# Attention and a maxout layer on one core: the first batch's queries in two parts, any free bank pair for any job, and a new order for every engine

## The chip, the cores and the metric

One NeuronCore of a Trainium2 chip. The five engines run their own instruction streams and wait for each other by semaphores: TensorE (PE) multiplies, ScalarE (ACT) takes exponentials, VectorE (DVE) moves, scales and transposes, GpSimd (POOL) casts, SyncE (SP) issues DMAs. The metric is device microseconds of one execution, lower is better.

## What is computed

Eight batches of eight heads, 1152 positions, head size 64. Queries are averaged in pairs, so 576 queries attend to 1152 keys. The result, 4608 tokens of 512 features, goes through a layer that takes the larger of two projections and projects back.

```python
q_pool = q.reshape(B, H, S // 2, 2, D).mean(axis=3)
scores = scale * np.matmul(q_pool, k.transpose(0, 1, 3, 2))
attn = softmax(scores)
attn_out = np.matmul(attn, v)
x = attn_out.transpose(0, 2, 1, 3).reshape(B * (S // 2), H * D)
g = np.maximum(x @ w1, x @ w2)
out = g @ w_out
```

Inputs and the output are float32; the kernel multiplies in bfloat16.

## The kernel before

**Attention.** A unit of work is a pair of heads: 8 batches x 4 = 32 head pairs, numbered 0 to 31. For each, queries are summed in pairs (`cast_q`, POOL), keys and values cast (`cast_k`, `cast_v`, POOL), and queries and keys transposed so that the head dimension lies on partitions. Keys of the first five pairs and queries of the first five are transposed by PE (`ktrans_pe`, `qtrans`, `qtrans0`) and copied out by VectorE; later keys by a DMA (`ktrans`), later queries by eight VectorE transposes (`qtrans_dve`). Scores are laid out as one long row of columns, pair after pair, key tile after key tile (9 tiles of 128 keys x 576 queries = 5184 columns, `PW`), and cut into groups of 512 columns: 324 groups, 10.125 a pair. `scores(g)` computes one group for both heads as row-tiled matmuls of 64 rows, which run side by side, into two PSUM banks, and ACT takes the exponential of both into `et` (line 591). When all groups of a pair are there, `av_jobs` multiplies them with the values: per head four chunks of 128 queries, nine matmuls each (line 495), and one remainder of 64 queries for both heads (line 507). A column of ones in the values gives the sum, VectorE divides (lines 517 to 525) into `xnat`, and `xtrans` (DMA) or `xtrans_pe` (PE, the first four pairs, the last of each batch in some stretches, and the last pair) transposes the result into `xT`.

**The layer.** max(a, b) = max(a - b, 0) + b, so the kernel forms `wd` = w1 - w2 (POOL), computes relu(x wd) (the h blocks, line 798 row-tiled in pairs of banks, line 771 singly at the end) and adds x (w2 w_out): `w21` = w2 w_out is made once on the chip (line 716) from w2 transposed by PE (line 687). The p blocks (lines 831 and 864) sum relu(x wd) w_out and x w21 for 128 or 256 tokens. An h block may begin only when all four head pairs of its tokens are in `xT`.

**Order.** A greedy planner (`choose`, `steady`, `refill` and a `table` of settings by time) makes the list of operations, with estimated costs. Then four strings written out by hand or by search (`pe_order` and so on, line 1413) give the order in which PE, VectorE, POOL and SP go through their lanes; `Plan.solve` places the semaphore waits. In `pe_order`, S is the next score group, a digit the next unit of the job in that PSUM bank, and y, z, Y, Z a fill: four dummy matmuls of 128 columns (line 319) that compute nothing that is used. There are 23 such letters, 7 of them at the start.

**PSUM.** Eight banks in four pairs. Scores use the three `sps` pairs in turn (`ring`) until the layer begins, then two of them; `fb` and the third `sps` pair hold the other jobs.

**First batch.** Pairs 0 to 3 are taken whole, one after the other. Only pair 0's queries are loaded and transposed in two parts, of 256 and 320 (`QA` = 256, `runs`):

```python
def runs(i):
    return ((0, QA), (QA, SQ)) if i == 0 else ((0, SQ),)
```

Of the kernel before, what the change touches and what calls it, by code (L numbers as in the profile page):

```python
# [7 lines left out]
P = 128  # L8
# [7 lines left out]

class Plan:

    INORDER = ("PE", "ACT", "DVE", "POOL")
    LAT = {"PE": 0.182, "ACT": 0.181, "DVE": 0.010, "POOL": 0.010}  # L20
    HEAR = {"PE": 0.046, "ACT": 0.024, "DVE": 0.024, "POOL": 0.075, "SP": 0.05}

    def __init__(self):
        self.ops = []
        self.writer = {}
        self.readers = {}
        self.free = {}
        self.dma_free = 0.0
        self.mode = None
        self.act_end = 0.0  # L30
        self.last = {}

    def deps(self, r, w, after=()):
        raw = {self.writer[k] for k in r if k in self.writer}
# [5 lines left out]
        return deps, raw  # L40

    def when(self, eng, r=(), w=(), after=(), fence=False):

        if any(k not in self.writer for k in r):
            return 1e9
        t = self.free.get(eng, 0.0)
        for d in self.deps(r, w, after)[0]:
            p = self.ops[d]
            if p["eng"] != eng or p["dma"] is not None or fence:
                t = max(t, p["seen"] + self.HEAR[eng])  # L50
        return t

    def op(self, eng, fn, r=(), w=(), dma=None, cost=0.1, mode="f", after=(), solo=False,
           fence=False):
        n = len(self.ops)
        assert all(k in self.writer for k in r), r
        deps, raw = self.deps(r, w, after)
        prev = self.last.get(eng)
        if prev is not None and (solo or self.ops[prev]["solo"]):
            deps.add(prev)  # L60
            raw.add(prev)
        self.last[eng] = n
        t = self.when(eng, r, w, after, fence)
        if dma is not None:
            if not self.dma_free:
                t = 0.78
            self.free[eng] = t + (1.3 if mode == "t" else 0.5)
            a = max(self.free[eng] + 1.2, self.dma_free)
            self.dma_free = a + cost + (0.9 if a < 5.0 <= a + cost else 0.0)
            seen = self.dma_free + 0.5  # L70
        else:
            if eng == "PE" and mode != self.mode:
                t = max(t, self.free.get("PE", 0.0) + 0.098)
                self.mode = mode
            busy = cost
            seen = t + cost + self.LAT[eng]
            if eng == "ACT":
                busy = cost + 0.051
                seen = max(seen, self.act_end + cost + 0.0735)
                self.act_end = seen  # L80
            elif eng == "DVE":
                busy = cost + 0.012
            self.free[eng] = t + busy
        self.ops.append(dict(eng=eng, fn=fn, deps=deps, raw=raw, dma=dma, w=tuple(w),
                             seen=seen, end=self.free[eng], solo=solo, fence=fence, r=tuple(r), at=n))
# [7 lines left out]
    def lane(self, o):  # L93
        key = (o["w"] or ("o",))[0]
        if o["eng"] == "PE":
            return "S" if key[0] == "s" else key[1:]
        if o["eng"] == "SP":
            return {"kT": "t"}.get(key[:2], key[0])
        if o["eng"] == "POOL":
            return {"kb": "k", "wd": "d"}.get(key[:2], key[0])  # L100
        for k in o["r"] + o["w"]:
            if k[0] == "f" and k[1:].isdigit():
                return k[1:]
        return {"qt": "T", "w2": "W", "wo": "W"}.get(key[:2], "Q")

    def reorder(self, want):

        ops = self.ops
        line = {}
        for n, o in enumerate(ops):  # L110
            line.setdefault(o["eng"], []).append(n)
        for eng, text in want.items():
            lanes = {}
            for n in line[eng]:
                lanes.setdefault(self.lane(ops[n]), []).append(n)
            assert sorted(c for c in text if c not in self.fill) == sorted(
                c for c, v in lanes.items() for _ in v)
            line[eng] = []
            for c in text:
                if c in self.fill:  # L120
                    m, mode, fn = self.fill[c]
                    key = f"f{m}"
                    nxt = ops[lanes[str(m)][0]]
                    n = len(ops)
                    ops.append(dict(
                        nxt, fn=fn, w=(key,), r=(), raw={self.writer["warm"]}, fence=False, at=n, inc=False, mode=mode, cost=0.0,
                        deps={d for d in nxt["deps"] if key in ops[d]["w"] and ops[d]["eng"] != eng}
                        | {self.writer["warm"]}))
                    nxt["deps"].add(n)
                    line[eng].append(n)  # L130
                else:
                    line[eng].append(lanes[c].pop(0))
        place = {}
        while len(place) < len(ops):
            before = len(place)
            for eng in line:
                while line[eng] and all(d in place for d in ops[line[eng][0]]["deps"]):
                    place[line[eng].pop(0)] = len(place)
            assert len(place) > before
# [5 lines left out]
    def solve(self):  # L145
# [3 lines left out]
        for n, o in enumerate(ops):  # L149
# [3 lines left out]
            for d in sorted(o["deps"], reverse=True):  # L153
                p = ops[d]
                if p["dma"] is None:
                    if p["eng"] == eng and not o["fence"] and (eng == "PE" or eng != "DVE" and d not in o["raw"]):
                        continue
# [29 lines left out]
    def emit(self, eng, h, sem, last_waits=()):  # L187
        for o in self.ops:
# [9 lines left out]
            inst = o["fn"](h)  # L198
# [8 lines left out]
class Job:  # L207


    def __init__(self, kind, units, evac, done=None, nb=None, single=None):  # L210
        self.kind, self.units, self.evac, self.done = kind, units, evac, done
        self.nb = nb
        self.single = single


def bass_funnel_attn__then__act_maxout2_kernel(
# [25 lines left out]
    assert NB == HP and NTOK % 512 == 0 and NT == 9 and B % 2 == 0  # L242
# [3 lines left out]
    NGR = NPAIR * PW // W  # L246

    ctx = ExitStack()
    with ctx:
# [6 lines left out]
        ident = sbuf([P, P], BF16, "ident")  # L256
        qraw = [sbuf([P, QU, 2, D], FP32, f"qraw{s}") for s in range(3)]
        kraw = [sbuf([P, 2, NT, D], FP32, f"kraw{s}") for s in range(3)]
        vraw = [sbuf([P, 2, NT, D], FP32, f"vraw{s}") for s in range(3)]
        qpw = [sbuf([P, QU, 2, D], BF16, f"qp{s}") for s in range(2)]  # L260
        qp = [t[0:HP, :, :, :] for t in qpw]
# [181 lines left out]
        def qtrans_dve(i, n):  # L443
# [9 lines left out]
            if n == 7:  # L453
                q_done.add(i)
# [1043 lines left out]
```

## Time and profile before

| what | value |
|---|---|
| median of three executions | 367.1 us (365.78, 367.1, 369.88) |
| profiled execution, span from first to last instruction | 368.9 us |
| exponentials, ACT | 307.6 us in 336 instructions |
| scores, PE | 121.5 us in 1162 matmuls |
| query transposes, VectorE | 101.3 us in 216 instructions |
| read from HBM, written | 62.91 MB, 9.44 MB |

The profile is of one execution on the chip. Busy times are unions of instructions on an engine; matmuls are pipelined and their ends are modelled, so a busy PE can still be one that loses time between matmuls. Views used below: the page's busy shares; windows, which give each engine's busy time within a stretch of the span; the timeline, in which neighbouring instructions of one kind are merged (start, length, engine, line, output and inputs, count); the waits; and the chain that ended last. The fill matmuls appear at line 319 and count as busy.

### The profile page before, as it was taken

What the parts mean: (1) busy time and instruction counts of PE and PEld (TensorE: products, weight loads), DVE (VectorE), ACT (ScalarE), POOL (GpSimd) and SP (SyncE); (2) the same over time, 40 slices, a digit from 0 to 9 for tenths busy, and PEclk for the clock granted to TensorE, in tenths of its full rate; (3) what the DMA queues carried; (4) which work ended last, traced back from release to release, by engine and by line L of the source; (5) the groups of instructions that cost most, each with busy time, mean ns of one, the idle gap of its engine ahead of it and who ended that gap; (6) DMA issues with size and microseconds to landing.
All of it is one profiled execution on the core that took longest, in us unless ns stands there. A gap on an engine that the chain in (4) does not pass through costs nothing.

```text
span 368.9 us, 13316 instructions
## 1 busy us (share of the span) xinstructions
PE 359.1 (97%) x5941; PEld 225.9 (61%) x5945; DVE 240.9 (65%) x521; ACT 315.6 (86%) x355; POOL 124.7 (34%) x111
## 2 busy tenths in 40 slices
PE   6999999999999999999999999999999999999996
PEld 5766564665556665657565665665666666556853
DVE  1478378867778867848885776577877766714411
ACT  4699989999999998999998999999999989895221
POOL 1256675533134333372242602525224440010000
PEclk9599999999999999999999999999999999999999
DMA  7999959999939998898999999998999680913206
GB/s 265 406 396 397 402 108 328 307 312 164 330 102 234 291 271 253 211 297 178 251 349 185 252 245 236 283 304 181 277 253 197 191 201 6 181 43 72 54 0 171
DMA packets 77640, 84.71 MB, mean 230 GB/s; under 512 B 49936, under 2 KB 50704, under 8 KB 77584
## 3 DMA queue, kind: packets, MB, share of 16 engines
q1 hardware_dynamic: 77024, 83.09, 84.8%
q8 instruction: 46, 0.75, 0.9%
q10 hardware_dynamic: 560, 0.79, 0.6%
q14 instruction: 10, 0.08, 0.1%
HBM read 62.91 MB, written 9.44 MB: 196 GB/s over the span
## 4 chain that ended last, share of the span: by engine, by line
PE 95%; DMA 2%; ACT 2%; issue 1%; SPq 0%; POOL 0%; DVE 0%; DVEq 0%
PE sps L584 22%; PE sps L495 12%; PE sps L831 11%; PE fb L831 10%; PE fb L495 9%; PE sps L798 8%; PE fb L798 7%; PE sps L864 3%; PE sps L507 2%; PE fb L716 2%; DMA kraw<-in_k_dram 2%; ACT et L591 2%; PE fb L507 1%; PE fb L864 1%; PE sps L771 1%; PE fb L319 1%
## 5 line engine op out<-in xcount | busy, mean ns | idle before, releaser
L591 ACT ACTIVATE et<-sps 128x1024 bf16<-128x1024 f32 (+1 forms) x336 | 307.6, 1002 | 25.1 <-PE sps L584 23.0
L584 PE MATMUL sps<-qpT,kT 64*128 64x256 bf16 (+7 forms) x1162 | 121.5, 287 | 1.0 <-issue 0.5
L449 DVE STREAM_TRANSPOSE qpT<-qp 32x288 bf16<-32x288 bf16 x216 | 101.3, 469 | 5.6 <-PE sps L584 1.5
L584 PEld LDWEIGHTS sps<-qpT,kT 64*128 64x128 bf16 x1162 | 49.6, 95 | 48.1 <-ACT et L591 15.8
L389 POOL TENSOR_TENSOR qp<-qraw 128x576 bf16<-128x576 f32 x30 | 42.1, 1406 | 98.2 <-DVE qpT L449 76.2
L395 POOL TENSOR_SCALAR vE<-vraw 128x1152 bf16<-128x1152 f32 x32 | 36.9, 1154 | 60.7 <-DMA vraw<-in_v_dram 60.7
L495 PE MATMUL sps<-vE,et 128*128 128x65 bf16 x1368 | 48.4, 193 | 0.0
L495 PEld LDWEIGHTS sps<-vE,et 128*128 128x128 bf16 x1368 | 43.6, 97 | 6.0 <-issue 5.3
L356 POOL TENSOR_SCALAR kbf<-kraw 128x1152 bf16<-128x1152 f32 x31 | 35.7, 1153 | 33.5 <-DMA kT<-kbf 16.5
L798 PE MATMUL sps<-xT,wd 64*128 64x512 bf16 (+3 forms) x368 | 43.7, 326 | 0.0
L831 PE MATMUL sps<-wo,stage 64*128 64x512 bf16 x256 | 36.8, 376 | 0.0
L495 PE MATMUL fb<-vE,et 128*128 128x65 bf16 x936 | 33.5, 193 | 0.5 <-issue 0.5
L798 PE MATMUL fb<-xT,wd 64*128 64x512 bf16 (+3 forms) x272 | 33.6, 333 | 0.1
L495 PEld LDWEIGHTS fb<-vE,et 128*128 128x128 bf16 x936 | 29.9, 97 | 5.5 <-issue 4.8
L831 PE MATMUL fb<-wo,stage 64*128 64x512 bf16 x224 | 33.0, 376 | 0.0
L807 DVE TENSOR_SCALAR stage<-sps 128x1024 bf16<-128x1024 f32 (+3 forms) x23 | 22.3, 969 | 15.7 <-PE sps L798 15.6
L798 PEld LDWEIGHTS sps<-xT,wd 64*128 64x128 bf16 x368 | 15.6, 94 | 13.7 <-PE sps L798 1.4
L807 DVE TENSOR_SCALAR stage<-fb 128x1024 bf16<-128x1024 f32 (+3 forms) x17 | 17.0, 999 | 10.7 <-PE fb L798 10.4
L517 DVE RECIPROCAL rc<-sps 128x5 f32<-128x5 f32 (+1 forms) x38 | 7.1, 186 | 19.7 <-PE sps L495 19.2
L831 PE MATMUL sps<-w,xT 64*128 64x512 bf16 x128 | 18.7, 377 | 0.0
L842 DVE COPY stage<-sps 128x1024 f32<-128x1024 f32 x8 | 9.8, 1225 | 12.8 <-PE sps L831 12.7
L831 PEld LDWEIGHTS sps<-wo,stage 64*128 64x128 bf16 x256 | 12.1, 94 | 9.5
(81 smaller groups left out, 296.6 us busy)
## 6 DMA issues: line engine op xcount, KB each, us to landing
vraw<-in_v_dram SPq DMA_DIRECT2D x32, 576.0 KB, 6.6
kraw<-in_k_dram SPq DMA_DIRECT2D x31, 576.0 KB, 6.6
qraw<-in_q_dram SPq DMA_DIRECT2D x31, 576.0 KB, 6.7
out_dram<-stage SPq DMA_DIRECT2D x21, 256.0 KB, 5.5
out_dram<-stage SPq DMA_DIRECT2D x23, 128.0 KB, 3.2
xT<-in_moe_w_dram SPq DMA_DIRECT2D x4, 512.0 KB, 10.7
stage<-in_moe_w_out_dram SPq DMA_DIRECT2D x4, 512.0 KB, 13.5
stage<-in_moe_w_dram SPq DMA_DIRECT2D x4, 512.0 KB, 13.1
```

Source lines behind the costliest of these rows:

```text
L356: op("POOL", lambda g: g.tensor_scalar(kbf[s][:, :, :, :].rearrange("p t h d -> p h t d"), kraw[r][:, :, :, :], 1.0, 1.0, ALU.mult, ALU.mu ...
L389: op("POOL", lambda g: g.tensor_tensor(qpf[s][:, :, :], qraw[r][:, :, 0, :], qraw[r][:, :, 1, :], ALU.add), r=[f"qraw{r}"], w=[f"qp{s}.0", ...
L395: op("POOL", lambda g: g.tensor_scalar(vE[r][:, :, :, 0:D].rearrange("p t h d -> p h t d"), vraw[r][:, :, :, :], 1.0, 1.0, ALU.mult, ALU.m ...
L449: op("DVE", lambda e: e.transpose(view[dst:dst + 32, :, 32 * pb:32 * pb + 32], qpf[s][src:src + 32, :, 32 * db:32 * db + 32]), r=[f"qp{s}. ...
L495: last = e.matmul(fb[m][:, sb * 66:sb * 66 + 65], et[:, a:a + P], vE[vs][:, t, half, 0:65], start=(t == 0), stop=(t == NT - 1))
L507: last = e.matmul(fb[m][rows(half), NCH * 66:NCH * 66 + 65], et[:, a:a + NB], vE[vs][:, t, half, 0:65], start=(t == 0), stop=(t == NT - 1))
L584: last = e.matmul(sps[r][:, h, col:col + hi - lo], kT[i % 3][rows(h), t, :], qpT[i % 3][rows(h), lo:hi], start=True, stop=True)
L591: op("ACT", lambda e: e.activation(et2[:, :, c:c + z - a], sps[r][:, :, a - g * W:z - g * W], EXP, scale=scale), r=[f"s{r}"], w=keys + ([f ...
L798: last = e.matmul(fb[m + k][:, 0:size], wd[z, ct, (f0 + k) * P:(f0 + k + 1) * P], xT[z, ct, n0:n1], start=(turn == 0 and ct == 0), stop=(t ...
L807: dve(lambda e: e.tensor_scalar_max(gT[:, f0:f0 + 2, g0:g0 + size], wide[m // 2][:, :, 0:size], 0.0), [f"f{m}", f"f{m + 1}"], w + [f"f{m}" ...
L831: last = e.matmul(fb[m + k][:, :], lhs, rhs, start=(turn == 0 and j == 0), stop=(turn == 1 and j == NC_ + NF - 1))
L864: return e.matmul(fb[m][:, 0:c1 - c0], lhs, rhs[:, c0:c1], start=(j == 0), stop=(j == NC_ + NF - 1))
```

## The change

Nearly the whole planner is replaced. The planner's choices, its settings and its lanes are gone; operations are created in program order with their dependencies, and a table lists, for each engine, the order of its operations by number, and for each of the eight banks, which jobs it holds in turn.

**Queries of the first batch.** Attention of batch 0 is done in eight blocks: queries 0 to 255 of pairs 0 to 3, then queries 256 to 575 of pairs 0 to 3. Later pairs stay whole. The result of the first four blocks is 256 tokens complete over all heads, so an h block of 256 tokens can begin there. The second parts have the remainder of 64 queries.

```diff
+        blocks = [(i, 0, QA) for i in range(NHP)] + [(i, QA, SQ) for i in range(NHP)] + [
+            (i, 0, SQ) for i in range(NHP, NPAIR)]
...
+        def av(n):
+            i, lo, hi = blocks[n]
...
+            c0, c1 = lo // P, min(hi // P, NCH)
+            tail = hi == SQ
+            j = plan.job("a", 2)
...
-        cuts = (0, 512, 1024, 1152, 1664, 2048, 2304, 2816, 3072, 3456, 3968, 4096, 4352, 4608)
+        CUTS = (0, 256, 512, 1024, 1152, 1664, 2048, 2304, 2816, 3072, 3456, 3968, 4096, 4352, 4608)
```

For this all four pairs' keys and values must stay until their second part: there are four `qpT`, and a fourth `kT` and `vE` lie in `xnat[1]`, which batch 1 does not write yet. Queries of pairs 0 to 3 are loaded, cast and transposed in two parts each, and `xtrans_pe` transposes the first batch in eight jobs, two a pair; after that only the last pair is transposed by PE.

```diff
-        qpT = [sbuf([P, SQ], BF16, f"qpT{s}") for s in range(3)]
+        xnat = [sbuf([P, NHP, NCH + 1, P], BF16, f"xnat{s}") for s in range(2)]
+        spare = xnat[1][:, :, :, :].rearrange("p a b c -> p (a b c)")
+        qpT = [sbuf([P, SQ], BF16, f"qpT{s}") for s in range(4)]
...
+        kT.append(spare[:, 0:NT * P].rearrange("p (t x) -> p t x", x=P))
...
+        vE.append(spare[:, NT * P:NT * P + NT * 132].rearrange("p (t h d) -> p t h d", h=2, d=66))
```

**Banks.** A job asks for one bank or a pair, and the table says which; score groups, attention products and the layer's jobs may all stand in any pair. The order string of PE now names banks: a to h is the next unit of the job in that bank, a capital a fill there.

```diff
+        for c in table["PE"]:
+            b = c.lower()
+            m = spots.index(b)
+            if c != b:
...
+                ops.append(dict(at=n, eng="PE", fn=None, deps={self.writer["ones"]} | used(m),
...
+            if not left[b]:
+                job = jobs[lists[b].pop(0)]
+                job.at = m
...
+    pe = (
+        "AAAAAAAAAAAAAAAAAaBbaceGGGGGGGGGgAAacHhgeFfagcefAAAageeeecadegfcefagceageeeeccacecgafgcaedgacaaegabc"
...
-        pe_order = (
-            "zzzzzzy0zz01SS0zzzSS0YSSYYSYYYS01SY0Sz0SSYSYY1S101S110SS000S1S01S01SSS000001S1S11SSS10SS101SS0S0"
```

Read with the lists of the banks, the new PE order begins: 17 fills, the first query transposes, a fill, two key transposes of pair 0, two score groups, 9 fills, the last key transposes of pair 0, 2 fills, two score groups, a fill, pair 1's key and query transposes, and so on. It has 34 fills in all. The first h block begins after 29 score groups; w21 starts after 40 and the first p block after 54. In the old order w21 starts after 32 groups, the first h block after 49 and the first p block after 69.

**Loads and casts.** SP's order begins with queries (first part) and keys of pair 0, then keys and first query parts of pairs 1 and 2, values of pair 0, keys of pair 3, the second query parts of pairs 0 and 1, the first of pair 3, and then weights between values. The old one took both parts of pair 0's queries among the first four loads, and weights from the sixth load on. The casts of w_out go from VectorE to POOL:

```diff
-                dve(lambda e: e.tensor_reduce(
-                    wo[:, 2 * ct:2 * ct + 2, :], wof[:, 2 * ct:2 * ct + 2, :].unsqueeze(3), AX.X, ALU.max),
...
+                op("POOL", lambda g: g.tensor_scalar(
+                    wo[:, 2 * ct:2 * ct + 2, :], wof[:, 2 * ct:2 * ct + 2, :], 1.0, 1.0, ALU.mult, ALU.mult),
```

The sizes of the matmuls, the number of exponentials' columns and the end of the kernel (single banks for the last tokens, the last block of 128 in 384 and 128 columns) stay.

More of the change, by code (lines that the diff above doesn't have):

```diff
@@ L39, in deps @@
             deps.update(self.readers.get(k, ()))
[L40 to L85, printed above, removed]
@@ L106, in reorder @@
[L106 to L132, printed above, removed]
@@ L135, in reorder @@
             before = len(place)
[L136 to L139, printed above, removed]
+            for e in line:
+                while line[e] and all(d in place for d in ops[line[e][0]]["deps"]):
+                    place[line[e].pop(0)] = len(place)
+            assert len(place) > before, {e: v[:1] for e, v in line.items()}
         for o in ops:
@@ new lines, in ecol, with ekeys, qkey @@
+        def ecol(n, t, at):
+            i, lo, hi = blocks[n]
+            return home[n] + t * (hi - lo) + at - lo
+        def ekeys(a, z):
+            return [f"e{x}" for x in range(a // GR, -(-z // GR))]
+        def qkey(i, lo):
+            return f"qpT{i % 4}.{'A' if lo < QA else 'B'}"
+        op("POOL", lambda g: g.memset(ident[:, :], 1.0), w=["id0"], cost=0.2)
+        op("POOL", lambda g: g.affine_select(
+            ident[:, :], ident[:, :], pattern=[[1, P]], compare_op=ALU.is_equal,
+            fill=0.0, base=0, channel_multiplier=-1), r=["id0"], w=["ident"], cost=0.3)
@@ L314, in fill, with vones @@
+        op("DVE", lambda e: e.memset(ones[:, :], 1.0), w=["ones"], cost=0.17)
+        def vones(g):
+            for s in range(4):
+                last = g.memset(vE[s][:, :, :, 64:66], 1.0)
+            return last
+        op("POOL", vones, w=[f"vE{s}" for s in range(4)], cost=0.33)
         def fill(m, mode):
```

1527 lines of the change are left out of this document (533 added, 994 removed), and 77 rows, old and new, of tables (act, bank_a, bank_c, bank_e).

## The prediction

> **What bounds the kernel now.** I read the page's busy shares first, then the chain that ended last.
>
> ```profile
> span 368.9 us, 13316 instructions
> PE 359.1 (97%) x5941; PEld 225.9 (61%) x5945; DVE 240.9 (65%) x521; ACT 315.6 (86%) x355; POOL 124.7 (34%) x111
> PE 95%; DMA 2%; ACT 2%; issue 1%; SPq 0%; POOL 0%; DVE 0%; DVEq 0%
> ```
>
> TensorE (PE) is busy 97% of the span and is 95% of the chain; ScalarE (ACT), which takes the exponentials, is second. The share is a mean over unlike stages, so next the table by stage (columns: length, then busy us of each engine, granted clock, DMA share, GB/s):
>
> ```profile
> 6.00:20.00 14.00, 11.83 (x140) 8.82 (x142) 4.98 (x10) 9.31 (x10) 3.55 (x4) 0.63 1.03 401
> 20.00:46.00 26.00, 24.48 (x469) 16.11 (x469) 17.74 (x33) 25.70 (x29) 16.84 (x14) 1.00 1.04 399
> 46.00:338.00 292.00, 290.82 (x5040) 178.45 (x5036) 207.97 (x453) 272.56 (x298) 103.40 (x85) 1.00 0.90 224
> 338.00:364.00 26.00, 25.79 (x252) 17.23 (x250) 8.85 (x22) 5.42 (x15) 0.00 (x0) 1.00 0.25 57
> ```
>
> Four regimes. From 6 to 20 us nobody is full: the granted clock is 0.63, and ACT is idle a third of the time. From 20 to 46 us ACT is the bound (25.70 of 26), with PE nearly full. From 46 us on PE is the bound (290.82 of 292), and after 338 us it works alone. Loads run at 400 GB/s until 46 us. So a change can help in two ways: more PE work done before 46 us, or less PE time after it. The early exponentials, from the timeline of ACT:
>
> ```profile
> 6.62 1.94 ACT L591 ACTIVATE et<-sps 128x1024 bf16<-128x1024 f32 x2 [1.65 <-PE sps L584]
> 10.14 1.94 ACT L591 ACTIVATE et<-sps 128x1024 bf16<-128x1024 f32 x2 [1.58 <-PE sps L584]
> 12.43 2.85 ACT L591 ACTIVATE et<-sps 128x1024 bf16<-128x1024 f32 x3 [0.36 <-PE sps L584]
> 15.84 1.02 ACT L591 ACTIVATE et<-sps 128x1024 bf16<-128x1024 f32 x1 [0.56 <-PE sps L584]
> 17.88 1.02 ACT L591 ACTIVATE et<-sps 128x1024 bf16<-128x1024 f32 x1 [1.02 <-PE sps L584]
> 19.47 26.50 ACT L591 ACTIVATE et<-sps 128x1024 bf16<-128x1024 f32 x29 [0.56 <-PE sps L584]
> 46.65 4.97 ACT L591 ACTIVATE et<-sps 128x1024 bf16<-128x1024 f32 x6 [0.69 <-PE sps L584]
> 52.12 12.19 ACT L591 ACTIVATE et<-sps 128x1024 bf16<-128x1024 f32 x13 [0.49 <-PE sps L584]
> ```
>
> Each is one group of 512 columns of two heads. The tenth starts at 19.47; from there one takes 26.50/29 = 0.914 us. Groups 21 and 41 cross the turn of the buffer and are split in two instructions, so 55 groups are begun in the 57 instructions shown, and the 56th is issued on PE at 63.8 us:
>
> ```profile
> 34.20 0.84 PE L584 MATMUL sps<-qpT,kT 64*128 64x448 bf16 x8
> 57.82 0.39 PE L798 MATMUL sps<-xT,wd 64*128 64x512 bf16 x2
> 63.75 0.38 PE L584 MATMUL sps<-qpT,kT 64*128 64x64 bf16 x4
> 361.42 3.19 PE L864 MATMUL sps<-wo,stage 128*128 128x512 bf16 x16
> 364.67 0.61 PE L864 MATMUL sps<-wo,stage 128*128 128x128 bf16 x8
> ```
>
> The first row holds groups 26 to 28, the 28th at about 34.7; the second is the first MoE matmul. PE ends at 365.3, 3.6 us before the span does.
>
> **PE's work, counted in both orders.** Unit times come from these rows (a row's length less one matmul's latency, over the matmuls less one):
>
> ```profile
> 30.69 1.53 PE L495 MATMUL fb<-vE,et 128*128 128x65 bf16 x45
> 30.28 0.47 PE L507 MATMUL fb<-vE,et 128*64 128x65 bf16 x18
> 336.11 1.68 PE L831 MATMUL fb<-wo,stage 64*128 64x512 bf16 x14
> 348.37 0.71 PE L771 MATMUL sps<-xT,wd 128*128 128x256 bf16 x5
> ```
>
> (1.53-0.19)/44 = 30.5 ns, so 0.274 us for nine attention-times-V matmuls; 17 ns in the remainder row; (1.68-0.38)/6 = 0.216 us for a pair of row-tiled 512-column matmuls, a score group being such a pair (0.218 with its pieces); (0.71-0.27)/4 = 0.11 us for 256 columns, so time goes with columns. With these, the order string before makes 321.0 us of PE work and the new one 320.8: the same matmuls, the first batch cut finer, 5 head pairs transposed by PE at the end of attention instead of 8. Work done when the 28th and the 56th group are issued: before 15.3 and 39.5, after 16.8 and 41.6 us. The early MoE block is what those 2.1 us are.
>
> After the 56th group, before has 321.0-39.5 = 281.5 us of work and takes 365.3-63.8 = 301.5. The 20.0 us between are not seen as waits; I put them on PE's changes between row-tiled 64-row matmuls, full ones and the 64-column remainder, counted in the order: 148 of them, 0.135 us each. From the 38th group (46.3 us, 23.8 us done, 162 changes) the same division gives 0.134. I take this price for both kernels. The whole orders have 231 and 230 changes, but after group 56 the new one has 163 against 148.
>
> **Part by part.** *Start, to the tenth group.* The new order puts 17 fill letters (68 dummy matmuls) before the first query transposes, where 28 matmuls stood, and 9 letters between the second group and the last key transposes of pair 0, where none stood.
>
> ```profile
> 1.10 3.17 PE L319 MATMUL fb<-xnat 128*128 128x128 bf16 x28 [1.10 <-DVE xnat L312]
> 4.20 0.42 PE L431 MATMUL fb<-ident,qp 64*64 64x64 bf16 x8
> 6.19 0.61 PE L584 MATMUL sps<-qpT,kT 64*128 64x256 bf16 x8 [0.19 <-DVE kT L471]
> 7.57 0.73 POOL L368 TENSOR_SCALAR kbf<-kraw 128x640 bf16<-128x640 f32 x1 [6.07 <-DMA kraw<-in_k_dram]
> 8.36 0.45 PE L464 MATMUL fb<-ident,kbf 128*128 128x128 bf16 x5 [1.56 <-POOL kbf L368]
> 9.49 1.04 PE L584 MATMUL sps<-qpT,kT 64*128 64x256 bf16 x8
> 9.87 1.15 POOL L356 TENSOR_SCALAR kbf<-kraw 128x1152 bf16<-128x1152 f32 x1 [1.57 <-DMA kraw<-in_k_dram]
> 13.89 1.27 PE L319 MATMUL fb<-xnat 64*128 64x128 bf16 x10
> 21.01 0.61 PE L319 MATMUL fb<-xnat 64*128 64x128 bf16 x8
> ```
>
> A dummy matmul takes 0.107 us at half clock ((1.27-0.31)/9) and 0.056 at full ((0.61-0.22)/7). The two eight-matmul rows of L584, 0.61 and 1.04, show the clock up by 6.2 us and down again by 9.5. With the rise at 5.9: 45 dummies cold (4.8 us) and 23 warm (1.3) end at 7.2, so the query transposes start there, not at 4.2, and the first exponential at about 9.1, not 6.62 (the same chain of 2.4 us less what the warm clock saves, plus one fill letter). Nine letters warm are 36 x 0.056 = 2.0 us: key transposes at 11.0, not 8.36; third exponential 12.4, not 10.14. The fifth group now belongs to pair 1 and needs its keys, whose cast starts at 9.87 at the latest (one load fewer stands ahead of them) and ends at 11.0; PE gets to their transposes at 12.5, two evacuations and the query evacuation follow, and the fifth exponential is at 14.6, not 12.43. From there, if PE keeps full clock, nothing interrupts ACT: the tenth starts at 14.6 + 5 x 0.914 = 19.2 against 19.47. **-0.3 us.** What was lost first is regained because before stopped for 0.56+1.02+0.56 us in that stretch.
>
> *Groups 10 to 28* are bound by ACT in both (18 x 0.914 = 16.5 us; PE's new work 11.2 + 28 changes 3.7 = 14.9): no change.
>
> *Groups 28 to 56.* Before took 63.8-34.7 = 29.1 us for 24.2 of work and 26 changes (3.5), so 1.4 us of it was waiting. After: 24.9 + 28 changes (3.7) = 28.6, above ACT's 25.6, so PE is the bound and the early MoE block fills what was idle. Bounds 28.6 (no waiting) to 30.0 (the same waiting); I take 28.9, near the lower, since the operands come in time: the last weight that the first block needs is the 23rd load, and these 23 hold 10.6 MB by their shapes, 27 us at 400 GB/s. **-0.2 us.**
>
> *After group 56:* work 320.8-41.6 = 279.2, changes 163 x 0.135 = 22.0, together 301.2 against 301.5. **-0.3 us.** The 2.1 us won are given back in 15 more changes.
>
> *At nothing:* the four casts of w_out go from VectorE (1.2 us each) to POOL (about 1.0 by the 1.15 of 1152 columns above): POOL is busy 16.84 of 26 us in that stage, and the w21 products that need them start at group 39, near 47 us. The queries of the first four pairs become eight loads, with more key loads ahead of weights: same bytes in a queue that stays full; a late one would show as an ACT wait and costs its length. More evacuations for the first batch: VectorE has a third of that stage free (17.74 of 26 busy). The tail after group 324 keeps its form.
>
> *Free banks.* The exponentials may now have three or four groups in flight; before, after the first batch, two. 13 bursts of three or four groups stand in the new order after group 64, none in the old. In such a burst PE waits if the pair isn't free:
>
> ```profile
> PE sps L584 <- ACT et L591: 0.3, 1, 0.3
> ```
>
> That is all PE waited for ACT before. Bounds: 0, or up to 0.4 each, 5 us; I take 0.4 in sum, near the row. An unexpected gain is excluded, since PE is already full there.
>
> Sum: -0.3 -0.2 -0.3 +0.4 = -0.4 us, a span of 368.5. The profiled execution's 368.9 lies 1.8 above the median of 367.1 (runs from 365.78 to 369.88); taken off the median, **366.7 us**.
>
> **Rivals.** *ACT unbroken from its start (faster).* The clock may rise up to 1.4 us sooner than 5.9, since more dummies stand in front; these then end near 5.9 and the first exponential is at 7.8. Pair 1's keys have 0.33 MB less ahead of them, 0.8 us at 400 GB/s: their cast may start at 9.0 instead of 9.87, and the fifth exponential 0.8 earlier than before's, at 11.6, the tenth at 11.6 + 4.6 = 16.2. That is -3.3; with -0.5 (28.6 us between groups 28 and 56), -0.3 and no waits in bursts **-4.1, 363.0**. For it: nine fill letters now cover the hole of 1.56 us, in which the clock was lost. Against: the same letters stand in front of the work whenever the keys land early.
>
> *The clock drops around group 5 (slower).* Before, it fell after the 1.56 us hole and came back shortly before 20 us:
>
> ```profile
> 6.00:8.00 2.00, 0.61 (x8) 0.25 (x8) 0.33 (x2) 1.38 (x2) 0.43 (x1) 1.00 1.00 375
> 18.00:20.00 2.00, 2.00 (x35) 1.23 (x34) 0.46 (x1) 1.44 (x2) 0.52 (x1) 0.62 1.03 402
> ```
>
> It was half for some 10 us. After, PE has little between the fifth and tenth group: 3.0 us of work in 4.6. If the clock is half from 12.5 to 22.7, groups 5 to 16 (5.6 us of work, 14 changes 1.9) take some 5.6 more than 7.5, against ACT's 10.1: with PE then waiting in turn for its transposes and evacuations, 3 to 5 us: **+4.3, 371.0**. It decides if a slice of 2 us shows PE busy for only 0.61 us or so, as 6 to 8 us did. The Trainium skill ("TensorE: Matmul & The Clock Gate", Part 1 and the table under "Why this matters for your kernels") has the clock fall only after a whole idle window, about 3.4 us. By that rule this rival would have no chance and its 0.14 would go to the forecast, whose 366.7 would stand. The trace does not agree: a hole of 1.56 us went before the fall.
>
> *The bursts wait (slower).* 13 x 0.4 = 5 us in place of the 0.4 of the sum: **+4.6, 371.3**. Against it: between groups 56 and 320 ACT has 264 x 0.914 = 241 us of work and PE some 260, so the banks are free again early on the whole. It decides where a burst begins while ACT still has a group in hand.
>
> **How the numbers follow.** Forecast 0.53, faster rival 0.18, clock drop 0.14, bursts 0.15. The forecast's own range is 364 to 369.5 (waiting 28.6 to 30.0, bursts 0 to 2.4). The runs before differ by 1.1%, and 1% is about what can be told from no change: faster means under 363.4, slower over 370.8. Three quarters of the faster rival lie past that bound, and of the forecast a few hundredths, where a start like the rival's meets an order without waits: 0.17 in all. The two slower rivals lie past theirs but for some 0.05, and the forecast adds 0.01: 0.25. Same 0.58. The range takes in the rivals' own centres: 363.0 to 371.3.
>
> **What would show it.** PE's total within 1 us of 359 plus some 3 for 44 added dummies, cold or warm; first exponential near 9.1, tenth at 19 to 19.5; no clock below 1 after 7 us; first MoE matmuls near 35 us, not 57.8; group 56 near 63.4. The forecast is wrong if ACT runs unbroken from before 12 us, if the stage from 46 to 338 us shows PE waits for ACT above 2 us, or if the changes cost other than 0.135.

## The result: slower by 12%, and the profile after

| | before | after |
|---|---|---|
| median of four executions beside each other | 367.51 us (365.78 to 369.88) | 410.31 us (408.94 to 412.74) |
| ratio | | 1.1186, 95% interval 1.1123 to 1.125 |
| span of the profiled execution | 368.9 us | 407.2 us (its time: 408.94 us) |

The forecast was 366.7, the range 363.0 to 371.3: wrong by some 44 us, and none of the rivals reaches that far. (In two later kernels, the last pairs by PE alone and with full dummies, the profiled one of four executions fell in a slower state; their medians leave it out.) The page of the kernel after, its span, busy shares and the engines of the chain that ended last:

```profile
span 407.2 us, 13616 instructions
...
PE 371.3 (91%) x6061; PEld 234.8 (58%) x6064; DVE 236.5 (58%) x539; ACT 313.8 (77%) x359; POOL 131.5 (32%) x121
...
PE 80%; issue 5%; ACT 4%; DMA 4%; SPq 3%; POOL 2%; DVE 2%; POOLq 0%
```

PE fell from 97% busy to 91%, and DMA, SP and POOL, 2% of the chain before, now hold 9% of it. What PE waited for (sum in us, times, longest):

```profile
PE ps L809 <- DMA xT<-xnat: 26.2, 4, 11.5
PE ps L598 <- ACT et L615: 1.2, 2, 0.7
```

Four waits, 26.2 us, all in an h block (line 809), all for a DMA that transposes attention's result; in the kernel before no wait of PE for such a DMA reached 0.2 us. PE's waits for ACT, which the bursts rival stood on, stayed near nothing. Behind the four, POOL's and SP's waits, first of the kernel before:

```profile
POOL kbf L356 <- DMA kT<-kbf: 16.5, 5, 7.4
...
SPq L330 <- POOL kbf L356: 8.2, 3, 5.0
```

and of the kernel after:

```profile
POOL kbf L507 <- DMA kT<-kbf: 144.2, 23, 11.4
...
SPq L464 <- POOL kbf L507: 57.1, 13, 6.9
```

The longest of the four waits in the timeline of after, SP's rows first, then POOL's, VectorE's and PE's (start, length, instruction, idle time before it):

```profile
191.81 2.08 SPq L533 DMA_TRANSPOSE kT<-kbf  x1
193.94 2.55 SPq L845 DMA_DIRECT2D out_dram<-stage  x4
196.53 0.59 SPq L473 DMA_DIRECT2D qraw<-in_q_dram  x1
200.62 0.39 SPq L464 DMA_DIRECT2D kraw<-in_k_dram  x1
201.05 1.31 SPq L839 DMA_DIRECT2D out_dram<-stage  x2
202.41 3.53 SPq L704 DMA_TRANSPOSE xT<-xnat  x2
...
199.44 1.15 POOL L507 TENSOR_SCALAR kbf<-kraw 128x1152 bf16<-128x1152 f32 x1 [7.51 <-DMA kT<-kbf]
...
196.06 0.42 DVE L670 TENSOR_TENSOR xnat<-ps,rc 128x256 bf16<-128x256 f32 x1
...
195.08 0.66 PE L809 MATMUL ps<-xT,wd 64*128 64x384 bf16 x6
207.25 0.50 PE L809 MATMUL ps<-xT,wd 64*128 64x384 bf16 x2 [11.50 <-DMA xT<-xnat]
```

Read it from the bottom. PE stops at 195.75 because the h block needs pair 15, the last pair of its batch. VectorE has that pair's result ready at 196.48. Its transposes are issued only at 202.41, since SP stands at a key load from 197.12 to 200.62; that load needs the key buffer that POOL's cast frees, and the cast began at 199.44, having waited 7.51 us for the key transpose of 191.81 to land and give back its `kbf` buffer. From 196.48 to 202.41 it is queueing, six microseconds; then five for two issues and the landing. The others end at 113.82, 250.54 and 294.37, took 4.9, 5.8 and 4.0 us, and are of pairs 7, 19 and 23.

How far the order of scores runs behind the kernel before, in us (issue of a group, from the trace): tenth +3.5, 56th +5.6, 171st +7.2, 181st +23.4, 221st +28.8, 261st +33.6, 324th +33.2. Most of it is lost in steps: at the start, and at the four waits.

### The profile page after: what moved, and what is told of

It reads as the page before. It is cut to its first block, busy times and chain, and to the rows that moved or that the text cites. A ratio compares the mean times of both kernels' runs of the same rounds, so it can differ in the third digit from the quotient of the medians.

```text
span 407.2 us, 13616 instructions
## 1 busy us (share of the span) xinstructions
PE 371.3 (91%) x6061; PEld 234.8 (58%) x6064; DVE 236.5 (58%) x539; ACT 313.8 (77%) x359; POOL 131.5 (32%) x121
## 4 chain that ended last, share of the span: by engine, by line
PE 80%; issue 5%; ACT 4%; DMA 4%; SPq 3%; POOL 2%; DVE 2%; POOLq 0%
PE ps L598 17%; PE ps L638 17%; PE ps L868 17%; PE ps L809 14%; ACT et L615 4%; DMA xT<-xnat 4%; PE ps L888 4%; PE ps L455 3%; PE ps L649 3%; PE ps L788 2%; PE ps L772 2%; SPq L704 1%; POOL qp L540 1%; DVE qpT L573 1%; POOL vE L584 1%
## 5 line engine op out<-in xcount | busy, mean ns | idle before, releaser
L615 ACT ACTIVATE et<-ps 128x1024 bf16<-128x1024 f32 (+5 forms) x340 | 305.4, 1009 | 60.4 <-PE ps L598 59.5
L598 PE MATMUL ps<-qpT,kT 64*128 64x256 bf16 (+7 forms) x1142 | 116.4, 287 | 1.7 <-ACT et L615 0.7
L809 PE MATMUL ps<-xT,wd 64*128 64x256 bf16 (+3 forms) x704 | 79.2, 330 | 27.3 <-DMA xT<-xnat 26.2
L507 POOL TENSOR_SCALAR kbf<-kraw 128x1152 bf16<-128x1152 f32 (+1 forms) x32 | 36.4, 1139 | 160.2 <-DMA kT<-kbf 144.2
L638 PE MATMUL ps<-vE,et 128*128 128x65 bf16 x2232 | 81.2, 193 | 0.0
L638 PEld LDWEIGHTS ps<-vE,et 128*128 128x128 bf16 x2232 | 71.7, 97 | 13.0 <-issue 11.8
L815 DVE TENSOR_SCALAR stage<-ps 128x512 bf16<-128x512 f32 (+3 forms) x44 | 39.9, 907 | 63.8 <-PE ps L809 63.3
L598 PEld LDWEIGHTS ps<-qpT,kT 64*128 64x128 bf16 x1142 | 47.3, 95 | 46.1 <-ACT et L615 16.3
L868 PE MATMUL ps<-wo,stage 64*128 64x512 bf16 x480 | 69.4, 380 | 0.0
L540 POOL TENSOR_TENSOR qp<-qraw 128x576 bf16<-128x576 f32 (+2 forms) x35 | 44.8, 1285 | 18.5 <-DVE qpT L573 17.9
L649 PEld LDWEIGHTS ps<-vE,et 128*64 128x64 bf16 x558 | 11.3, 111 | 10.2 <-issue 5.3
```

The costliest lines, as they stand in the source:

```text
L507: op("POOL", lambda g: g.tensor_scalar(dst, src, 1.0, 1.0, ALU.mult, ALU.mult), cost=0.02 + 0.126 * (hi - lo), **io)
L540: op(eng, lambda e: e.tensor_tensor(qp[s][:, lo:hi, :], qraw[z][:, lo:hi, 0, :], qraw[z][:, lo:hi, 1, :], ALU.add), r=[f"qraw{z}.{u}" for ...
L598: last = e.matmul(wide[m // 2][:, h, col:col + hi - lo], kT[slot(i)][rows(h), t, :], qpT[i % 4][rows(h), lo:hi], start=True, stop=True)
L615: op("ACT", lambda e, m, col=col, at=at, n=n: e.activation(et2[:, :, at:at + n], wide[m // 2][:, :, col:col + n], EXP, scale=scale), r=[f" ...
L638: last = e.matmul(fb[m + half][:, c * 66:c * 66 + 65], et[:, a:a + P], vE[s][:, t, half, 0:65], start=(t == 0), stop=(t == NT - 1))
L649: last = e.matmul(fb[m][rows(half), NCH * 66:NCH * 66 + 65], et[:, a:a + NB], vE[s][:, t, half, 0:65], start=(t == 0), stop=(t == NT - 1))
```

## The experiments

Times are medians; the sets ran on different chips, and the kernel before, run beside each, lay at 366.1 to 367.2 every time. A time without a ratio is one execution. An expected span is that of the profiled execution, some 2 us less than its time.

### The last pair by PE, or first on SP

Before, PE transposes the results of pairs 0 to 3, 31 and also 7, 11 and 15; after, of 0 to 3 and 31. The first kernel gives the last pair of every batch to PE, also 19, 23 and 27, which the kernel before had on the DMA too:

```diff
-    K_PE, Q_PE, XPE = 5, 5, (NPAIR - 1,)
+    K_PE, Q_PE, XPE = 5, 5, (7, 11, 15, 19, 23, 27, 31)
```

> In the changed kernel PE waited four times, 26.2 us in all, in the first h block after the end of a batch, for the DMA that transposes the last pair's result. Here the last pair of six more batches is transposed by PE, as pairs 0 to 3 and 31 are; nothing else moves. Theory (the result of a batch's last pair comes too late by DMA): the four waits go, and with them some 7 us at half clock that followed them; span 370 to 377 against 407.2, and 46 to 338 us without PE waits over 1 us. Rival (bursts and mode changes of the new order cost the time, the waits only stand in their place): span above 392, and waits of PE for ACT or VectorE appear instead. What stays over 368.9 should be the start, 5.6 us late at group 56.

394.73 us, ratio 1.072 (1.0658 to 1.0784): 16 us won, half of the 30 to 37 expected. The theory holds in part: in the profiled execution the waits for pairs 7 and 15 are gone, but PE still waits at two h blocks, now for the DMA transposes of other pairs:

```profile
PE ps L809 <- DMA xT<-xnat: 11.8, 2, 6.6
```

The second leaves the transposes on the DMA and moves them ahead on SP; in the order of SP, for pair 7 (650 and 651; 455 and 456 are stores, 1222 a key load, 1453 a query load), and likewise for pairs 11, 15, 19 and 27 (ahead of those of pair 23 stood no store or key load):

```diff
-... 455 456 1222 650 1453 651 ...
+... 650 651 455 456 1222 1453 ...
```

> The changed kernel with one edit on SP's list: the two DMA transposes of each batch's last pair stand ahead of the stores and key loads that stood directly before them, some of which wait. If the lateness is made by SP's queue, the longest wait of 11.5 us (where a key load held SP for 4 us and the transposes were issued 6 us after their data) falls to about 5, the four together from 26.2 to 10 to 16 us, span 390 to 396. If it is made by the transposes' own time to landing (4.3 us median), the waits stay within 3 us of 26.2 and the span at 403 to 408. Rival (bursts, mode changes): the same 403 to 408.

403.43 us, a span of 401.7, and the waits:

```profile
PE ps L809 <- DMA xT<-xnat: 18.9, 4, 6.4
```

That lies between the two cases: what stood directly ahead of them on SP is worth 7 us of the waits and 5.5 of the span, and most of the lateness is made elsewhere.

### The dummies at the start

A fill takes the row mode of the operation that follows it, 64 rows for all of the 17 leading ones. One line makes all of them use 128 rows:

```diff
-            z = slice(0, P) if mode == "f" else rows(0)
+            z = slice(0, P)
```

> The changed kernel with dummy matmuls of 128 rows everywhere; its first 68 had 64 rows, and its clock rose at 14.5 us, where the 28 of before had 128 and it rose by 6.2. If 64-row dummies do not lift the clock, it rises here by 8 us: the 68 dummies end near 7.2 instead of 8.5, the 36 after the second group take 2.0 instead of 3.85, the tenth group is issued near 19.5 instead of 22.4, and the span falls by 2 to 4 us to 403 to 405. If the clock rises for another reason (its own phase, or real data), it rises at 11 us or later as before and the span stays within 1.5 us of 407.

404.64 us, a span of 402.9: 4.3 us won, near what was expected. The timeline of PE in the kernel after:

```profile
1.10 7.43 PE L455 MATMUL ps<-ones 64*128 64x128 bf16 x68 [1.10 <-DVE ones L441]
...
10.03 1.03 PE L598 MATMUL ps<-qpT,kT 64*128 64x256 bf16 x8 [0.17 <-DVE kT L524]
11.00 3.85 PE L455 MATMUL ps<-ones 128*128 128x128 bf16 x36
...
15.72 0.61 PE L598 MATMUL ps<-qpT,kT 64*128 64x256 bf16 x8
```

and with full dummies:

```profile
1.10 6.52 PE L455 MATMUL ps<-ones 128*128 128x128 bf16 x68 [1.10 <-DVE ones L441]
...
8.69 0.63 PE L598 MATMUL ps<-qpT,kT 64*128 64x256 bf16 x8 [0.15 <-DVE kT L524]
9.25 2.18 PE L455 MATMUL ps<-ones 128*128 128x128 bf16 x36
```

Eight score matmuls take 1.03 us at half clock and 0.61 at full (rows of before in the prediction). After 7.43 us of 64-row dummies the clock was still half, and it rose only at 14.5, near the end of the 36 full-row ones. The same test from the other side, the kernel before with its leading fills in 64 rows:

```diff
-            "zzzzzzy0zz01SS0zzz
+            "ZZZZZZY0ZZ01SS0zzz
```

> The kernel before with its first 36 dummies of 64 rows instead of 128, nothing else. If 64-row dummies do not lift the clock, it is not full at 6 us: the 8 matmuls of the first two groups take about 1.0 us instead of 0.61, and the clock rises only after 14 us; the total moves by no more than 3 us, since ACT and the loads bound this stretch. Rival (the clock follows real data or phase): the first two groups take 0.61 as before.

366.87 us, the time of its profiled execution. Its first score groups ran at half clock, and the clock rose at 8.4 us, sooner than the 14 expected:

```profile
1.10 3.16 PE L319 MATMUL fb<-xnat 64*128 64x128 bf16 x28 [1.10 <-DVE xnat L312]
...
6.29 1.04 PE L584 MATMUL sps<-qpT,kT 64*128 64x256 bf16 x8 [0.17 <-DVE kT L471]
...
7.77 1.16 PE L319 MATMUL fb<-xnat 128*128 128x128 bf16 x12
8.86 0.61 PE L584 MATMUL sps<-qpT,kT 64*128 64x256 bf16 x8
```

So the half rows cost the new order more than the old, because 17 letters of them stand in front of the work. One run could be chance, but all runs agree: in the five kernels that begin with 68 dummies of 64 rows the clock rose at 11.9 to 14.5 us, in the ten that begin with full rows at 3.7 to 7.0. And this execution never lost the clock again, where the profiled one of before ran at half for 10.2 us from 9.3 on: its tenth group is 4.2 us earlier, its span 364.4. My base, the span of 368.9, held those 4 us.

### The key loads

In the kernel after, from pair 12 on, each key load is moved on SP to the place behind the next key transpose (973 is a key load, 782 a key transpose):

```diff
-... 868 873 920 973 782 ...
+... 868 873 920 782 973 ...
```

> The changed kernel with one edit on SP's list: from pair 12 on, each key load stands directly behind the next key transpose instead of ahead of it. Taking the last pairs' transposes to PE removed 14 us of the 38 and left two waits of 5.2 and 6.6 us for transposes of other pairs. In that run SP stood still from 210.6 to 218.3 us at a key load whose buffer a POOL cast frees only after an earlier key transpose has landed (10 us after its issue), with the result transposes queued behind it. Theory now: this stop of SP at key loads, 57 us in 13 waits, is what makes the result transposes late. Then the waits of PE for them fall from 26.2 to under 10 us and the span to 375 to 388. Rival (the transposes' own time to land makes them late): waits 20 us or more, span over 398.

389.42 us, 21 us won, with no operation changed. Then the three together, and the same with 7 leading fill letters for 17:

```diff
-        "AAAAAAAAAAAAAAAAAaBbaceG
+        "AAAAAAAaBbaceG
```

> The last pairs by PE, the key loads later, and dummy matmuls of 128 rows: all three edits together. If the three causes are the whole of it, the span is that of the kernel before less the better clock at the start, give or take the 68 + 36 dummies: 364 to 372, no PE wait over 2 us after 46 us. If bursts and mode changes cost something of their own, the span stays at 375 or more with no wait for DMA left.

> As the one with the three edits together, with 7 letters of dummies at the start instead of 17, as in the kernel before. If the 68 dummies stand in front of the first query transposes, the first group is issued near 6.5 us instead of 8.8 and the span falls by another 1.5 to 2.5 us; if ACT and the loads bound the start anyway, by less than 0.7. Against the kernel before: between 0.99 and 1.01.

379.26 and 376.89 us (ratio 1.0309, 1.0262 to 1.0356): both over what was expected, though PE's waits for the result DMA were gone in both. So the first meets its second case: something beside the three causes costs the new order time. The table further down says what that can be.

Does the place of the load explain it alone? In the kernel before, 14 key loads (k) are moved forward, directly behind the key transpose (t) ahead of them:

```diff
-            "xqtxvvxtqovoxtkoxoxkqokotqtvq
+            "xqtxvvxtqovoxtkkkoxoxqootqtkvq
```

> The kernel before with 14 of its key loads moved forward on SP, each directly behind the key transpose ahead of it; nothing else. Theory: the place of the key load on SP alone makes the waits: SP stands at these loads until POOL has cast (its wait for kbf from 8.2 to over 40 us), result transposes of the batches whose last pair goes by DMA come late, PE waits for xT over 4 us in sum, and the time is 371 to 387. Rival: before's casts run early enough on POOL (16.5 us of waiting for kT in all), so that SP hardly stops there: within 365 to 369, and then it is the late cast on POOL, not the place of the load alone, that the change brought.

367.11 us, ratio 1.0011 (0.9984 to 1.0038). The rival: SP loses nothing at an early key load if the casts run early. POOL's and SP's waits there:

```profile
POOL kbf L356 <- DMA kT<-kbf: 14.3, 4, 7.6
...
SPq L330 <- POOL kbf L356: 5.3, 2, 4.2
```

### The buffer that the cast waits for

So the suspect is the cast. It writes one of two `kbf` buffers and must wait until the DMA transpose of two pairs ago has read it. A third buffer, all orders as they are (for room, the ones that dummies read lie in a part of `rc` that is written late):

```diff
-        kbf = [sbuf([P, NT, 2, D], BF16, f"kbf{s}") for s in range(2)]
+        kbf = [sbuf([P, NT, 2, D], BF16, f"kbf{s}") for s in range(3)]
...
-            s, z = i % 2, i % 3
+            s, z = i % 3, i % 3
```

> The kernel after with a third buffer for the cast keys (kbf), all orders as they are; the ones for the dummies lie in an unused part of rc. Theory: VectorE's and TensorE's waits begin on POOL: a key cast waits for the DMA transpose that still reads its kbf buffer (144.2 us in sum, longest 11.4), the key load waits for the cast (57.1 us on SP), and the result transposes stand behind the load. With a third buffer the cast waits for a transpose one pair older: POOL's sum falls below 60 us, SP's wait for casts below 25, PE's for xT from 26.2 below 12, and the time is 380 to 394. Rival: the DMA transposes themselves are slow or late (the order has them late, or they contend): POOL's wait goes, but PE waits for xT as before, and the time stays over 402.

386.45 us, ratio 1.0511 (1.0432 to 1.0589): 24 us from 2304 bytes a partition. (In the profiled execution 26.6 us are won after the 56th group and 3.3 lost before it, where PE stands for 3.6 us at 52 to 56 us; the trace does not say for what.) The waits of POOL, SP and PE in this kernel:

```profile
POOL kbf L507 <- DMA kT<-kbf: 3.1, 3, 2.1
...
SPq L464 <- POOL kbf L507: 2.6, 2, 2.3
...
PE ps L809 <- DMA xT<-xnat: 3.2, 2, 2.2
```

144.2, 57.1 and 26.2 us became 3.1, 2.6 and 3.2, without a transfer or a place in the order changed. That the DMA transposes are slow or late in themselves, the rival, is out for these waits.

The trace says why two buffers were enough before. From pair 5 on, medians: before, a key transpose is issued 5.7 us after its cast, and the cast that needs the same buffer starts 11.6 us after that issue. After, the transpose comes 16.1 us after its cast and the next cast 6.4 us after the issue, with the transfer taking 6.0: it starts the moment the buffer is free.

### Whether the causes add

The PE pairs, and the moved key loads, each with full dummies:

> The kernel after with the last pair of each batch transposed by PE and dummies in all 128 rows; key loads where they are. With full dummies alone it is 404.6, with the PE pairs alone 395.1. If the start and the pairs are separate causes the gains add: 388 to 391. If the one hides in the other's waits: 392 or more. Beside the run with key loads moved as well (379.3) it gives the price of the key loads once the last pairs no longer wait for the DMA: 9 to 12 by the sums so far; under 5 if only those pairs were hurt by them.

> The kernel after with the key loads moved behind the next key transpose and dummies in all 128 rows; the last pairs by DMA. With the key loads alone it is 389.4. Additive: 382 to 385, with PE's waits for xT near 8.7 in sum; then the pairs by PE are worth 3 to 6 more (to 379.3). Rival (what the start wins is lost again in later waits, as 5.7 of it was not): 387 to 390.

392.8 us (1.0635 to 1.0806) against 394.73, and 389.59 (1.0505 to 1.0683) against 389.42: the start, worth 4 to 6 us by itself, was worth nothing here that stands out from the noise. The third buffer with full dummies and 7 fill letters:

> The kernel after with the third kbf buffer, 7 leading fill letters in place of 17, and dummies in all 128 rows. Theory: the start and the late key casts are the two causes and add here, since with the third buffer nearly no wait for the DMA is left in which the start's gain could vanish: the 56th group at 63 to 67 us (72.67 with the buffer alone), 307 to 308.5 us from there to TensorE's end as with the buffer alone, together 373 to 379 us and 2 to 3% above the kernel before. Rival: the start's gain is lost again, as it was beside the moved key loads (389.42 against 389.59): 384 to 388. Neither has it below the kernel before: the orders still end with more changes between row modes than before's (167 against 150 after the 56th group).

384.1 us (1.0404 to 1.0528), the rival again, against 386.45 with the buffer alone. The 56th group came at 63.15 us in place of 72.67, but the 101st at 118.20 in place of 118.86: 9 us vanished, 5.2 of them in a longer wait for pair 7's result (7.38 us, 2.19 with the buffer alone), the rest in a wait of 1.84 us for VectorE at 76.5 and in half clock after both. From its timeline, and its windows (busy us of the engines, granted clock, DMA share, GB/s):

```profile
102.70 0.60 SPq L464 DMA_DIRECT2D kraw<-in_k_dram  x1
103.36 1.54 SPq L704 DMA_TRANSPOSE xT<-xnat  x1
104.94 1.14 SPq L473 DMA_DIRECT2D qraw<-in_q_dram  x1
106.13 1.21 SPq L704 DMA_TRANSPOSE xT<-xnat  x1
...
113.32 0.61 PE L809 MATMUL ps<-xT,wd 64*128 64x512 bf16 x2 [7.38 <-DMA xT<-xnat]
```

```profile
95.00:100.00 5.00, 5.00 (x114) 3.50 (x112) 3.69 (x9) 5.00 (x6) 1.55 (x2) 1.00 1.03 277
100.00:105.00 5.00, 4.52 (x114) 3.38 (x110) 4.79 (x13) 5.00 (x8) 1.15 (x1) 1.00 1.19 243
105.00:110.00 5.00, 0.94 (x10) 0.27 (x8) 1.09 (x4) 1.90 (x3) 3.64 (x3) 1.00 1.21 371
```

The DMA engines are full (share over 1) and what PE waits for is issued behind loads and lands 7 to 8 us after its issue: who comes earlier waits longer. The last two kernels take this wait away in two ways, by PE for all last pairs, and by the place on SP, both with the third buffer and the mended start:

> The kernel after with the third kbf buffer, the last pair of each batch transposed by PE, 7 leading fill letters and dummies in all 128 rows; no load is moved. Theory (late casts and last pairs through the DMA are the whole cause, the start the rest): no wait of PE for xT above 1 us, the stage from group 56 to TensorE's end 302 to 306 us (work 280.6, 173 changes of row mode, small gaps), group 56 at 63 to 65, the time 371 to 377 us. Rival (a third cause, such as the loaded DMA queues, makes another transfer late as soon as these are gone): waits over 4 us in sum and 380 or more.

> The kernel after with the third kbf buffer, 7 leading fill letters, dummies in all 128 rows, and on SP the last pairs' result transposes ahead of the stores and key loads in front of them; they stay on the DMA. If they are issued too late: the waits for xT, 9.4 us in sum before this move, fall below 3, and the time is 373 to 378. If they land too late whenever they are issued (4.3 to 9.4 us after the issue in that stretch): the wait at 106 us stays above 4 us and the time is 380 or more.

377.43 us (1.0251 to 1.0353) and 378.24 us (1.0259 to 1.0361), both just over the range of their theories. In the first no wait for the result DMA is left, but the stage from the 56th group on takes 308.7 us, not 302 to 306; in the second:

```profile
PE ps L809 <- DMA xT<-xnat: 4.3, 2, 3.6
```

Between the two cases: the transposes of pair 7 were issued too late, and at the earlier place 3.6 us of the wait for them are still left. No kernel made from the new one reaches the one before.

## Why the prediction was wrong

**The step that failed** is "*After group 56*": "work 320.8-41.6 = 279.2, changes 163 x 0.135 = 22.0, together 301.2". It makes PE's time out of PE's work and its changes of row mode, and puts PE's waits for a DMA at nothing without a reason. The stage took 334.5 us: 26.2 of the excess are the four waits, and some 7 are half clock that came with them. Behind the waits stand two things that the prediction named and did not follow up. *At nothing* has the casts of w_out and more loads on POOL and SP, but not that both queues have a new order, in which the key transposes come 10 us later after their casts. And "5 head pairs transposed by PE at the end of attention instead of 8" went into the sum as work saved, without what the transposes pass through on the DMA: their place on SP, the transfer, the h block that needs a batch's last pair. The first weighs more: with the third buffer, and the pairs still on the DMA, the waits fell from 26.2 to 3.2 us. Only pairs 7, 11 and 15 went over to the DMA, pair 11 made no wait, and pairs 19 and 23, with two of the four waits, were on the DMA before as well and made none there. A row of before that shows such a wait, POOL's 16.5 us for a `kbf` buffer, stood in the waits of that kernel and was not used.

By the runs: the third buffer alone won 24 us, all last pairs by PE alone 16, full-row dummies alone 4 to 6; the three together, with 7 leading letters, from 410.31 to 377.43, give 33, as they share waits. With the buffer and the start mended, the last pairs by PE are worth 7 (384.1 to 377.43).

**Start, to the tenth group: -0.3 forecast, +3.5 measured.** The step "45 dummies cold and 23 warm end at 7.2" took the clock to rise at 5.9 as before. The 68 are 64-row dummies, end at 8.5, and the clock rises at 14.5. First exponential 10.7 us, not 9.1; the h blocks began at 40.8, not near 35. The rivals at this place, ACT unbroken and a drop around group 5, both need a warm clock there and did not come about.

**Groups 10 to 56: -0.2 forecast, +2.1 measured.** Groups 10 to 28 took 16.5 us as forecast, but before's took 15.8; groups 28 to 56 took 30.5 where 28.9 was forecast. This part stays open.

**After group 56: -0.3 forecast, +33.0 measured**, and here the terms that the sum did have were good. PE's stage from the 56th group to its end, with the forecast's work, the changes of row mode counted in each trace (148 and 163 in the forecast; a pair's transposes count as full rows), and all idle times of PE above 0.3 us. The price of a change, 0.128 us, is set so that before comes out: (301.5 - 281.5 - 0.8) / 150.

| kernel | work | changes | idle over 0.3 us | sum | measured |
|---|---|---|---|---|---|
| before | 281.5 | 150 | 0.8 | 301.5 | 301.5 |
| after | 279.2 | 167 | 27.1 | 327.7 | 334.5 |
| third buffer | 279.2 | 167 | 5.6 | 306.2 | 307.9 |
| third buffer, PE pairs, start | 280.9 | 173 | 4.9 | 307.9 | 308.7 |

(280.9 is 279.2 and 30 transposes of 0.056.) The 6.8 us that after has over the sum are its clock: it was half for 23.9 us in four stretches that begin in the waits or at their end, 15 of them with PE at work, which lose some 7.4. The third buffer's 1.7 are likewise a stretch of 3.4 us. So the work and the changes of row mode stand as forecast within a few microseconds; the waits were missing. That a change of row mode as such costs 0.128 us isn't shown: the price is set in one kernel and fits three others, but no run changes their number alone. With it, the table also accounts for what is left in the kernel of the last row: 7 us over before in this stage, of them 2.3 from more changes and PE transposes than the saved work pays for, 4.1 from small gaps, 0.8 unexplained. An early MoE block that gains was seen in no run: the 56th group of that kernel comes at 62.70, and at 60.20 and 59.51 in the two kernels made from before, both without the stretch at half clock, 9.3 to 19.5 us, of the profiled execution of before.

**The bursts** were rightly taken as nearly nothing: 1.2 us. **The base** was mis-sized: the profiled 368.9 held a stretch at half clock, and the runs beside it mostly span 364 to 366; "taken off the median" hid that in the sum but not in the start, where the forecast measured itself against a slow tenth group.

Not tried: an order with the key transposes issued earlier and only two buffers.

## What to carry to other kernels

When an order is made anew, cost the queues that look idle: for each buffer handed from an engine to a DMA, ask how long after its writing the transfer is issued, how long it lands, and when the next writer comes; where the next writer comes sooner than the transfer lands, everything queued behind it waits, here through POOL and SP up to TensorE. Work taken off the busiest engine and given to a DMA is not saved before the consumer's order leaves the landing time free (here 2.2 to 7.2 us from issue, median 4.3, and the queue before it). And a gain ahead of a late transfer can be worth nothing until that transfer is mended.

## What the runs showed of the hardware that was not expected

**64-row dummies did not lift the clock.** 7.43 us of them left it at half; with 128 rows it was up at 6.5 us. The ten full-row starts rose 2.6 to 5.9 us after the first dummy, the five with 68 half-row ones 10.8 to 13.4 after it. The Trainium skill ("TensorE: Matmul & The Clock Gate", Part 1) has it that "The warm-up budget is ~3.4 µs of time, not a number of matmuls"; the full-row starts lie around that time, the 64-row starts do not, so the rows in use count too.

**The granted clock of a row isn't the clock before the first record.** The windows of the kernel after give 1.00 here, while 36 dummies in 3.85 us are 0.107 us each, the half-clock time:

```profile
10.00:12.00 2.00, 1.97 (x18) 1.41 (x19) 0.19 (x1) 1.32 (x2) 1.88 (x3) 1.00 1.04 398
12.00:14.00 2.00, 2.00 (x22) 2.00 (x20) 0.00 (x0) 0.62 (x1) 0.00 (x0) 1.00 1.05 406
```

The length of a known matmul tells it; "no clock below 1 after 7 us", which I named as a sign, failed for the four later stretches but could not have shown the start.

**A short hole can cost the clock, or not.** It fell after idle times of PE of 1.84 us (third buffer with the mended start, at 76.5 us) and of 2.19 (third buffer alone, at 114.4), and not after 1.86 and 2.10 at the place of the 1.84 in the last two kernels. Each drop lasted 3.41 us or a multiple, and so did the stretches at full clock between them: 98.99, 81.92, 37.55 and 40.96 us in the kernel after are 29, 24, 11 and 12 times 3.41. So within a run the clock changes at steps of that length; whether a hole's place within such a step decides was not tested.
